# Two decode layers on one core: the last 2 KB of each row of three V loads per layer moved into short loads of their own

## The chip, the core and the metric

The kernel runs on one core of a Trainium2 chip. The metric is device time in microseconds (us), the median of several executions. A profiled execution gives the trace from which the durations below come.

## The reference

Two identical layers are run one after the other on a batch of four single tokens (decode): attention over a cache of 4096 keys and values, then a gated feed-forward block. Everything is float32.

```python
def _A_ref(x, k_cache, v_cache, wq, wo):          # x: 4 x 1 x 512
    q = (x @ wq).reshape(4, 1, 32, 128).transpose(0, 2, 1, 3)
    k = jnp.repeat(k_cache, 4, axis=1)             # k_cache, v_cache: 4 x 8 x 4096 x 128
    v = jnp.repeat(v_cache, 4, axis=1)
    scores = jnp.einsum("bhqd,bhkd->bhqk", q, k) * (128 ** -0.5)
    p = _softmax(scores, axis=-1)
    o = jnp.einsum("bhqk,bhkd->bhqd", p, v)
    return o.transpose(0, 2, 1, 3).reshape(4, 1, 4096) @ wo
def _B_ref(x, w1, w3, w2):                         # w1, w3: 512 x 1792, w2: 1792 x 512
    return (_silu(x @ w1) * (x @ w3)) @ w2
for _ in range(2):                                 # the same caches and weights in both layers
    x = x + _A_ref(_layernorm(x), k_cache, v_cache, wq, wo)
    x = x + _B_ref(_layernorm(x), w1, w3, w2)
```

The caches are by far the largest operands: K and V are 64 MB each, and both layers read both.

## The kernel before

The work of a layer runs over the eight KV heads, here called groups. For each group the core needs an 8 MB block of K and an 8 MB block of V. Each block is laid out in device memory as 128 rows of 64 KB, one row to a partition, so that one load (`nc.sync.dma_start`) fetches it whole. K block of group n gives the scores (`scores`, 32 matmuls of 512 columns on TensorE, L337); the softmax is taken from them (`factors`, `exponents`); V block of group n then gives the weighted sum (`weigh`, 32 matmuls on L380, in two halves of 16 with a copy of the first half by ScalarE between them, L387).

All loaded data lives in one SBUF tile, `arena`, 214 KB to a partition. A list `plan` holds every load of the program in order with the work that reads it. `pump` (L123 to L137) walks this list: as soon as room for the next entry is free in `arena` it writes the load into the program, always on SyncE (SP). `done` gives room back when the last reader of an entry has been written, and calls `pump` again. The order on SP is therefore the order of the plan, and SP works through it strictly in order: a load that must wait holds up every load behind it.

In the middle of layer 0 the arena holds one K block at 128 to 192 KB and one V block at 64 to 128 KB. The loads go K(n+1), V(n), K(n+2), V(n+1). K(n+1) may be issued when the scores of group n have read the K block that lies in its place, V(n) when `weigh` of group n-1 has read V(n-1). In layer 1 the groups run in reverse, 7 to 0, and the blocks of K move through the arena, but the alternation is the same.

Each load adds to a semaphore when its data has landed. SP's loads use eight such semaphores, DMAHW0 to DMAHW7, in turn. The program lets a load start only when the load that used the same semaphore before it, eight loads earlier, has landed. These waits, and those for room in `arena`, are what `[waits ...]` shows in the rows below (PE_49 is TensorE's own counter).

The line that issues the loads is L128:

```python
a = take(n, at)
if a is None:
    return
nc.sync.dma_start(arena[:, a * KB:(a + n) * KB], src)
```

Of the kernel before, what the change touches and what calls it, by code (L numbers as in the profile page):

```python
# [29 lines left out]
KB = 256  # L30
# [2 lines left out]
AGAIN = (0,)  # L33
SPLIT = 3
SCRATCH = 64


@with_exitstack
def tile_decode_layers(ctx: ExitStack, tc: tile.TileContext, x, kt, v, wq, wo, w1, w3, w2, out):
    nc = tc.nc  # L40
# [5 lines left out]
    arena = const.tile([P, ARENA * KB], F32, name="arena")  # L46
# [5 lines left out]
    def take(n, at=None):  # L52
        if at is not None and at < WO:
            return at
        for i, (lo, size) in enumerate(free):
            a = lo if at is None else at
            if lo <= a and a + n <= lo + size:
                free[i:i + 1] = [(p, s) for p, s in ((lo, a - lo), (a + n, lo + size - a - n)) if s]
                return a
        return None  # L60
# [60 lines left out]
    def pump():  # L121
        while state["next"] < len(plan):
            src, per, keys, at = plan[state["next"]]  # L123
            n = src.shape[-1] // KB
            a = take(n, at)
            if a is None:
                return
            nc.sync.dma_start(arena[:, a * KB:(a + n) * KB], src)  # L128
            i = state["next"]
            if i == 0:  # L130
                nc.sync.dma_start(xt[:8], x[:8])
            left[i] = (len(keys), a, n)
            for j, key in enumerate(keys):
                where[key] = (a + j * per, per, i)
            state["next"] += 1
# [5 lines left out]
    def done(*key):  # L141
        i = where[key][2]
        k, a, n = left[i]
        left[i] = (k - 1, a, n)
        if k == 1:
            give(a, n)
            pump()

    def vacate(*key):
        a, n, _ = where[key]  # L150
        give(a, n)
        pump()

    xt = const.tile([P, KC, B], F32, name="xt")
    nc.scalar.dma_start(xt[8:], x[8:])
    pump()

    ident = const.tile([P, P], F32, name="ident")
# [410 lines left out]
```

## Time and profile before

| | |
|---|---|
| time, median of 3 runs | 709.03 us (708.67 to 710.82) |
| the profiled execution | 710.14 us |
| its span, first to last instruction | 708.4 us |
| TensorE matmuls busy | 412.7 us, 58% of the span |
| VectorE / ScalarE busy | 78.0 us / 38.3 us |
| data moved by DMA | 299.89 MB in 13860 packets |
| mean granted TensorE clock | 0.793 |

How to read what follows: times are us from the start of the span unless marked ns. SPq is SP issuing. In the chain of waits a line is a start, a duration and what took that time; `DMA arena<-in_v` is a load of V, counted from its issue until the work that waited for it could go on. In a table by windows, each engine has its busy time and number of instructions, then come the granted TensorE clock, the mean busy share of the core's 16 DMA engines and the rate. A packet's whole time is put into the window in which it starts, so the share can come out over 1.00 in a short window. In the page's list of DMA issues a row gives the number of such loads, the KB of each and the median time from issue to landing.

### The profile page before, as it was taken

Reading aid. Unit: us, or ns where it says so; the run is one execution under the profiler, and the core shown is the slowest. Engines: PE = TensorE matmul, PEld = TensorE weight load, DVE = VectorE, ACT = ScalarE, POOL = GpSimd, SP = SyncE. Lnnn points to the kernel's source line nnn. Section 1 sums busy time; section 2 is a strip of 40 time slices with the busy share of each in tenths; the row PEclk is TensorE's granted clock in tenths of the full one; section 3 lists DMA queues with packets and bytes.
Section 4 is the critical chain, followed back from the end, with each engine's and each line's share of the span. In section 5 each row is a group of like instructions: output and inputs, shape, how many; then the busy total and the mean of one; then the engine's idle time right before and its main releaser. Section 6 shows DMA issues by size and latency. Waiting matters only on the chain.

```text
span 708.4 us, 7205 instructions
## 1 busy us (share of the span) xinstructions
PE 412.7 (58%) x3250; PEld 146.1 (21%) x3250; DVE 78.0 (11%) x270; ACT 38.3 (5%) x87; POOL 2.9 (0%) x10
## 2 busy tenths in 40 slices
PE   4455453546564564547778895365564645466677
PEld 2112021212121121212243321021121212121235
DVE  2001010101001000101011111010010101010111
ACT  0000000000000000002010000000000000000101
POOL 0000000000000000000000000000000000000000
PEclk9866687767778777778899998588797878788869
DMA  9999999999999999999999999999999999999996
GB/s 385 459 404 466 415 419 460 418 427 455 415 433 449 418 438 444 415 426 421 412 391 393 410 445 426 455 423 419 459 419 426 449 426 427 448 410 424 428 423 255
DMA packets 13860, 299.89 MB, mean 423 GB/s; under 512 B 1671, under 2 KB 1799, under 8 KB 6151
## 3 DMA queue, kind: packets, MB, share of 16 engines
q1 hardware_dynamic: 13696, 299.44, 98.9%
q8 instruction: 25, 0.41, 0.2%
q10 hardware_dynamic: 135, 0.01, 0.0%
q14 instruction: 4, 0.03, 0.0%
HBM read 299.38 MB, written 0.07 MB: 423 GB/s over the span
## 4 chain that ended last, share of the span: by engine, by line
DMA 73%; PE 22%; another core or an unknown queue 2%; ACT 1%; issue 1%; DVE 0%; SPq 0%; ACTq 0%
DMA arena<-in_v 52%; PE o_ps L380 16%; DMA arena<-in_w 9%; DMA arena<-in_wq 6%; DMA arena<-in_wo 3%; DMA arena<-in_kt 3%; PE s_ps L337 2%; PE q_ps L281 2%; ACT p L387 1%; PE m_ps L292 0%; PE t_ps L281 0%; PE x_ps L479 0%; SPq L128 0%; PE x_ps L401 0%
## 5 line engine op out<-in xcount | busy, mean ns | idle before, releaser
L380 PE MATMUL o_ps<-arena,pT 128*32 128x512 f32 x1024 | 150.6, 738 | 150.2 <-DMA arena<-in_v 136.6
L337 PE MATMUL s_ps<-arena,qpad 128*32 128x512 f32 x1024 | 149.7, 739 | 80.6 <-DMA arena<-in_kt 80.6
L380 PEld LDWEIGHTS o_ps<-arena,pT 128*32 128x32 f32 x1024 | 38.1, 131 | 259.7 <-issue 226.6
L337 PEld LDWEIGHTS s_ps<-arena,qpad 128*32 128x32 f32 x1024 | 39.4, 132 | 174.8 <-issue 161.7
L389 DVE SCALAR_TENSOR_TENSOR p<-o_ps,parts,p 128x512 f32<-128x512 f32 x16 | 12.0, 750 | 274.2 <-PE o_ps L380 249.2
L344 DVE TENSOR_REDUCE top<-s_ps 128x1 f32<-128x512 f32 x16 | 11.1, 691 | 191.8 <-PE s_ps L337 191.8
L392 PE MATMUL m_ps<-sel,p 128*128 128x16 f32 x128 | 17.0, 265 | 14.3 <-DVE p L389 14.2
L281 PE MATMUL q_ps<-arena,xpad 128*32 128x512 f32 x112 | 16.0, 696 | 11.6 <-DMA arena<-in_wq 11.6
L401 PE MATMUL x_ps<-arena,oT 128*4 128x256 f32 x256 | 18.7, 434 | 5.5 <-DMA arena<-in_wo 3.6
L392 PEld LDWEIGHTS m_ps<-sel,p 128*128 128x128 f32 x128 | 15.5, 191 | 29.2 <-DVE p L389 29.2
L387 ACT ACTIVATE p<-o_ps,parts 128x512 f32<-128x512 f32 x16 | 11.0, 687 | 193.4 <-PE o_ps L380 185.5
L368 PE MATMUL t_ps<-ident,p 128*128 128x128 f32 x64 | 10.9, 295 | 13.5 <-ACT p L362 13.5
L355 ACT ACTIVATE f<-d 128x1 f32<-128x1 f32 x16 | 3.2, 203 | 252.6 <-DVE d L353 252.6
L362 ACT ACTIVATE p<-s_ps,top 128x512 f32<-128x512 f32 x16 | 11.0, 684 | 81.7 <-PE m_ps L392 81.7
L225 PE MATMUL d_ps<-ident,rows 128*32 128x128 f32 x70 | 12.2, 277 | 0.0
L369 DVE COPY pT<-t_ps 128x512 f32<-128x512 f32 x16 | 11.1, 691 | 8.4 <-PE t_ps L368 8.4
L368 PEld LDWEIGHTS t_ps<-ident,p 128*128 128x128 f32 x64 | 7.0, 145 | 18.3 <-ACT p L362 15.3
L423 PE MATMUL s_ps<-arena,xpad 128*32 128x192 f32 (+1 forms) x128 | 9.3, 412 | 1.9 <-DMA arena<-in_w 1.5
L423 PE MATMUL o_ps<-arena,xpad 128*32 128x192 f32 (+1 forms) x128 | 8.1, 360 | 2.3 <-DMA arena<-in_w 2.2
L401 PEld LDWEIGHTS x_ps<-arena,oT 128*4 128x4 f32 x256 | 6.2, 94 | 14.4 <-issue 4.6
L225 PEld LDWEIGHTS d_ps<-ident,rows 128*32 128x32 f32 x70 | 7.5, 111 | 3.6
L281 PEld LDWEIGHTS q_ps<-arena,xpad 128*32 128x32 f32 x112 | 3.7, 126 | 21.6 <-DMA arena<-in_wq 12.7
(92 smaller groups left out, 130.4 us busy)
## 6 DMA issues: line engine op xcount, KB each, us to landing
arena<-in_kt SPq DMA_DIRECT2D x4, 4096.0 KB, 21.0
arena<-in_v SPq DMA_DIRECT2D x4, 4096.0 KB, 38.8
arena<-in_kt SPq DMA_DIRECT2D x9, 1024.0 KB, 10.2
arena<-in_w SPq DMA_DIRECT2D x15, 512.0 KB, 7.1
arena<-in_wq SPq DMA_DIRECT2D x1, 7168.0 KB, 39.5
arena<-in_v SPq DMA_DIRECT2D x3, 2048.0 KB, 39.3
arena<-in_wo SPq DMA_DIRECT2D x1, 4096.0 KB, 24.1
arena<-in_kt SPq DMA_DIRECT2D x2, 2048.0 KB, 19.9
```

What stands on the lines that cost most here:

```text
L225: nc.tensor.matmul(d_ps[0:32, :], rows, ident, start=True, stop=True)
L281: nc.tensor.matmul(ps[32 * k:32 * k + 32, :], xpad[:, k, lo:lo + 32], w[:, k, :], start=first, stop=last)
L337: nc.tensor.matmul(s_ps[32 * b:32 * b + 32, :], qpad[:, b, lo:lo + 32], k[:, j, :], start=(blk == 0), stop=(blk == NB - 1))
L344: nc.vector.tensor_reduce(top[:, 0:1], s_ps, axis=AX.X, op=ALU.max, negate=True)
L368: nc.tensor.transpose(t_ps[:, i, :], p[:, i * P:(i + 1) * P], ident)
L369: nc.vector.tensor_copy(pT.rearrange("p i r -> p (i r)"), t_ps.rearrange("p i r -> p (i r)"))
L380: nc.tensor.matmul(o_ps[32 * b:32 * b + 32, :], pT[:, i, 32 * b:32 * b + 32], w[:, b, :], start=(i == 0), stop=(i == NI - 1))
L387: nc.scalar.activation(p, o_ps, AF.Copy, scale=st["parts"][:, 0:1])
L389: nc.vector.scalar_tensor_tensor(p, o_ps, st["parts"][:, 1:2], p, op0=ALU.mult, op1=ALU.add)
L392: nc.tensor.matmul(flat(m), p[:, j * P:(j + 1) * P], sel[:, j].rearrange("p h b -> p (h b)"), start=(j == 0), stop=(j == 3))
L401: nc.tensor.matmul(x_ps[r:r + B, e * 256:e * 256 + 256], left(2 * i + n), w(n)[:, e * 256:e * 256 + 256], start=first, stop=last)
L423: nc.tensor.matmul(ps[32 * j:32 * j + 32, lo:lo + n], x32[:, k, :], w[:, j * n:(j + 1) * n], start=(k == 0), stop=(k == KC - 1))
```

## The change

A table `SHARES` names three V loads per layer: groups 2, 3 and 4 in layer 0 and groups 5, 4 and 3 in layer 1. For these, `pump` loads 62 KB of each row with the main load and the last 2 KB with short loads that each cover a run of rows: 15, 14, 13, 12, 10 and 64 rows for the first of the three; 11, 9, 7, 5 and 96 for the second; 8, 6, 4, 3, 2, 1, 8 and 96 for the third. They are written right behind the main load, on SP too. The bytes, their places in `arena` and all computation stay as they were.

```diff
+SHARES = {}
+for layer, groups in ((0, (2, 3, 4)), (1, (5, 4, 3))):
+    for g, c in zip(groups, ((15, 14, 13, 12, 10, 64), (11, 9, 7, 5, 96), (8, 6, 4, 3, 2, 1, 8, 96))):
+        SHARES["v", layer, g, 0] = c
...
-            nc.sync.dma_start(arena[:, a * KB:(a + n) * KB], src)
             i = state["next"]
+            rows_of = SHARES.get(keys[0], ())
+            m = n - 2 if rows_of else n
+            nc.sync.dma_start(arena[:, a * KB:(a + m) * KB], src[:, 0:m * KB])
+
+            r = 0
+            for c in rows_of:
+                nc.sync.dma_start(arena[r:r + c, (a + m) * KB:(a + n) * KB], src[r:r + c, m * KB:])
+                r += c
```

The first place is SP in layer 0, around the V load of group 4 (the third load of the three). Before, from V of group 3 on, then K5, V4, K6, V5, K7, V6:

```order
L128 DMA arena<-in_v 128x16384 [waits DMAHW5_49,DMAHW3_49,PE_49]
L128 DMA arena<-in_kt 128x16384 [waits DMAHW4_49,PE_49]
L128 DMA arena<-in_v 128x16384 [waits DMAHW5_49,PE_49]
L128 DMA arena<-in_kt 128x16384 [waits DMAHW6_49,PE_49]
L128 DMA arena<-in_v 128x16384 [waits DMAHW7_49,PE_49]
L128 DMA arena<-in_kt 128x16384 [waits DMAHW0_49,PE_49]
L128 DMA arena<-in_v 128x16384 [waits DMAHW1_49,PE_49]
```

K6 follows directly on V4 there. The same stretch of the changed program, K5, V4 with its eight short loads, K6, V5:

```order
L135 DMA arena<-in_kt 128x16384 [waits DMAHW2_49,PE_49]
L135 DMA arena<-in_v 128x15872 [waits DMAHW3_49,PE_49]
L139 DMA arena<-in_v 8x512 [waits DMAHW4_49,PE_49]
L139 DMA arena<-in_v 6x512 [waits DMAHW5_49]
L139 DMA arena<-in_v 4x512
L139 DMA arena<-in_v 3x512 [waits DMAHW6_49]
L139 DMA arena<-in_v 2x512 [waits DMAHW7_49]
L139 DMA arena<-in_v 1x512 [waits DMAHW0_49]
L139 DMA arena<-in_v 8x512 [waits DMAHW1_49]
L139 DMA arena<-in_v 96x512 [waits DMAHW2_49]
L135 DMA arena<-in_kt 128x16384 [waits DMAHW3_49,PE_49]
L135 DMA arena<-in_v 128x16384 [waits DMAHW4_49,DMAHW5_49,DMAHW2_49,DMAHW6_49,DMAHW1_49,DMAHW7_49,DMAHW0_49,PE_49]
```

K5 is counted on DMAHW1 here, V4's main load on DMAHW2 and the first seven short loads on DMAHW3 to DMAHW7, DMAHW0 and DMAHW1. The eighth short load, of 96 rows, comes round to DMAHW2 and waits on it; K6 stands behind that load. The other two V loads have five and six short loads, which do not come round to their own main load. In layer 1 the place looks the same at V of group 3: its eighth short load waits on the semaphore of its own main load, and the next K load stands behind it.

The second place is TensorE around `weigh` of the same group 4, which stands behind the scores of group 5. Before:

```order
L337 MATMUL s_ps<-arena,qpad 32x512 [waits DMAHW6_49,DVE_49]
L337 MATMUL s_ps<-arena,qpad 32x512 x31
L380 MATMUL o_ps<-arena,pT 32x512 [waits DMAHW7_49,DVE_49]
L380 MATMUL o_ps<-arena,pT 32x512 x15
L380 MATMUL o_ps<-arena,pT 32x512 [waits Activation_49]
L380 MATMUL o_ps<-arena,pT 32x512 x15
```

And in the changed program:

```order
L348 MATMUL s_ps<-arena,qpad 32x512 [waits DMAHW1_49,DVE_49]
L348 MATMUL s_ps<-arena,qpad 32x512 x31
L391 MATMUL o_ps<-arena,pT 32x512 [waits DMAHW2_49,DVE_49]
L391 MATMUL o_ps<-arena,pT 32x512 x15
L391 MATMUL o_ps<-arena,pT 32x512 [waits Activation_49]
L391 MATMUL o_ps<-arena,pT 32x512 x14
L391 MATMUL o_ps<-arena,pT 32x512 [waits DMAHW4_49,DMAHW5_49,DMAHW3_49,DMAHW6_49,DMAHW2_49,DMAHW7_49,DMAHW1_49,DMAHW0_49]
```

The last 2 KB of a row feed one matmul alone, the last of the 32 in `weigh`; it now waits for all the short loads, and the 31 before it wait for the main load only.

## The prediction, made before the changed kernel ran

> **What bounds the kernel now.** First the page's busy times and the chain that ended last.
>
> ```profile
> span 708.4 us, 7205 instructions
> PE 412.7 (58%) x3250; PEld 146.1 (21%) x3250; DVE 78.0 (11%) x270; ACT 38.3 (5%) x87; POOL 2.9 (0%) x10
> DMA packets 13860, 299.89 MB, mean 423 GB/s; under 512 B 1671, under 2 KB 1799, under 8 KB 6151
> q8 instruction: 25, 0.41, 0.2%
> DMA 73%; PE 22%; another core or an unknown queue 2%; ACT 1%; issue 1%; DVE 0%; SPq 0%; ACTq 0%
> ```
>
> No engine is busy for more than 58% of the span, while 73% of the chain is loads. The windows of three whole groups, the two in front of the third changed load of layer 0 and the one in front of that of layer 1, say how hard the loads run:
>
> ```profile
> core 0: us, PE busy (x) PEld busy (x) DVE busy (x) ACT busy (x) POOL busy (x), PEclk, DMA share, GB/s
> 159.50:198.20 38.70, 19.80 (x142) 6.44 (x142) 3.89 (x12) 1.67 (x4) 0.00 (x0) 0.76 1.00 434
> 198.20:236.90 38.70, 20.35 (x142) 6.55 (x142) 3.89 (x12) 1.67 (x4) 0.00 (x0) 0.76 1.00 434
> 540.60:579.30 38.70, 21.94 (x158) 7.03 (x158) 3.89 (x12) 1.67 (x4) 0.00 (x0) 0.76 1.00 432
> ```
>
> The DMA share is 1.00 and TensorE works 20 to 22 us of each 38.7 us. So the DMA engines are the bound, and a group costs the 16 MB that it moves at 434 GB/s. A microsecond in which they have nothing to do is a microsecond at the end. They never run dry, because the next load is queued long before the last one has landed:
>
> ```profile
> 209.16 0.33 SPq L128 DMA_DIRECT2D arena<-in_v  x1
> 226.30 0.33 SPq L128 DMA_DIRECT2D arena<-in_kt  x1
> 209.16 27.72 DMA arena<-in_v
> 236.89 0.14 issue
> 551.05 28.25 DMA arena<-in_v
> 569.02 0.33 SPq L128 DMA_DIRECT2D arena<-in_kt  x1
> ```
>
> The first two rows and the last are from the timeline, the others from the chain. V4 is issued at 209.16 and lands at 236.89; K6, behind it on SP, is issued at 226.30, so 236.89 - 226.30 = 10.6 us before V4 is in. V3 of layer 1 lands at 551.05 + 28.25 = 579.30, and the K load behind it was issued at 569.02, 10.3 us earlier. That lead keeps the share at 1.00.
>
> **The wait that the change adds.** In the changed program the eighth short load of these two V loads waits until its own main load has landed, since both use one semaphore, and the next K load stands behind it on SP. K6 can then be issued at 236.9 instead of 226.3. Everything issued earlier has landed by then: six of the other short loads were queued with V4, the seventh at K5's landing, one 8 MB load or 19 us before. So the DMA engines are empty from V4's last byte until the new issue brings bytes. This happens once a layer. The other V loads with five and six short loads reach back no further than to a load that landed a group ago.
>
> How long the engines stand empty is not shown before; the nearest rows are a load on an empty queue at the start and the store at the end:
>
> ```profile
> arena<-in_wq SPq DMA_DIRECT2D x1, 1024.0 KB, 4.9
> out<-p SPq DMA_DIRECT2D x1, 64.0 KB, 1.6
> 1.10:1.70 0.60, 0.00 (x0) 0.00 (x0) 0.36 (x1) 0.27 (x1) 0.21 (x1) 1.00 0.00 0
> 1.70:2.30 0.60, 0.00 (x0) 0.00 (x0) 0.56 (x7) 0.60 (x1) 0.00 (x0) 1.00 1.24 218
> 0.74 0.38 SPq L128 DMA_DIRECT2D arena<-in_wq  x1
> ```
>
> The gap consists of the time from last byte to landing plus that from issue to first byte, which is what issue to landing takes beyond moving the data. For the store it is 1.6 - 0.15 (64 KB at 434 GB/s) = 1.45 us; for the first load 4.9 - 2.4 (1 MB) = 2.5 us. The windows agree: issued at 0.74, no byte by 1.70, then only half the rate. The changed place is a load, but not the first of a program, so I take 1.9 us, between the two. The 0.33 us that SP needs for the 96-row load before it can issue K6 lies beside that load's own data, 192 KB or 0.45 us. **Two gaps: +3.8 us**, bounds +2.9 and +5.0.
>
> Nothing covers a gap. TensorE's slack doesn't help, as loads set the pace. TensorE itself isn't held by the short loads: the 31 matmuls before the last need the main load alone,
>
> ```profile
> 237.02 5.75 PE o_ps L380 x32
> 247.29 28.41 DMA arena<-in_v
> ```
>
> and `weigh` runs from 237.02 to 247.29, while the 96 rows land some 2.4 us after 236.9. If they came after 247 instead, V5's issue would slip too; 8 us of cover are left. V5 at 247.29 only queues behind K6.
>
> **The short loads themselves.** There are 6 + 5 + 8 = 19 more loads a layer. On a full queue the price of a small load shows where loads of 512 KB and 1 MB follow each other:
>
> ```profile
> 350.50:358.50 8.00, 7.50 (x114) 4.04 (x106) 0.94 (x5) 0.47 (x2) 0.00 (x0) 1.00 1.03 411
> 403.00:419.00 16.00, 13.14 (x102) 3.98 (x106) 2.97 (x10) 1.56 (x4) 0.00 (x0) 0.89 1.02 429
> L128 SPq DMA_DIRECT2D arena<-in_v x21: 327/328/432, 30.4 to 639.5; - x21
> ```
>
> 411 instead of 434 GB/s over 8 us is 0.42 us lost on 6.3 loads, 0.07 us a load; 429 over 16 us is 0.18 us on 6.5 loads, 0.03. Nineteen loads in two layers at most 0.07 each would be 2.7 us if every one occupied all engines, but 16 of 19 have at most 15 rows and touch only some; the three wide ones a layer give 6 x 0.03 to 0.07 = 0.2 to 0.4. I take **+0.2**, ends 0 and +1.0. SP's 0.33 us for each issue, 2.6 us for eight, lie inside the 17 us from V4's issue to K6's.
>
> **Who carries the rows.** A load of n rows below 16 can't occupy 16 engines evenly, so the short loads shift load between engines. At one row an engine, the 16 such loads of a layer give an engine 0 to 16 rows where an even split of their 128 rows gives 8. A 2 KB row costs 2 KB / (423/16 GB/s) = 0.08 us, so an engine gains or loses at most 0.62 us a layer. Whether that helps depends on who is late, and engines are apart:
>
> ```profile
> 700.00:701.00 1.00, 1.00 (x29) 0.81 (x32) 0.18 (x1) 0.00 (x0) 0.00 (x0) 1.00 0.61 244
> 701.00:702.00 1.00, 1.00 (x32) 0.97 (x28) 0.00 (x0) 0.00 (x0) 0.00 (x0) 1.00 0.46 178
> 703.00:704.00 1.00, 0.71 (x12) 0.47 (x13) 0.00 (x0) 0.00 (x0) 0.00 (x0) 1.00 0.13 47
> 704.00:704.60 0.60, 0.60 (x28) 0.60 (x24) 0.00 (x0) 0.00 (x0) 0.00 (x0) 1.00 0.09 34
> ```
>
> Behind the last load some engines are through before 701 and one or two run until 704.6, a lag of about 4 us; the 25 instruction fetches of q8, 16 KB each, are a likely source. No view names the late engines. If the short loads relieve them in both layers they gain 1.25 us; if they burden them they lose as much. I take **0**, ends -1.25 and +1.25.
>
> [...]
>
> A gap also makes all engines start level again. Lag that one engine had collected before it is paid there, and another may be last afterwards: at least 0, and at most about the price of a fetch or two a gap, 1.2 us (16 KB at 26 GB/s is 0.6). I take **+0.2** for both, ends 0 and +1.2.
>
> **The sum.** 3.8 + 0.2 + 0 + 0.2 = +4.2 us. On the profiled execution, span 708.4 and 710.14 in all (1.7 around the span), that is a span of 712.6. That execution lies 1.1 us over the median of 709.03; the forecast for the median is **709.0 + 4.2 = 713.2 us**. The ends of the terms together are 2.9 + 0 - 1.25 + 0 = +1.65 and 5.0 + 1.0 + 1.25 + 1.2 = +8.45.
>
> **Rivals.**
> 1. The gaps are there but short, about the store's 1.45 us each, and the shifted rows help a little: 2.9 - 1.0 = +1.9, 710.9 us, not to be told from no change (a measurement of this kernel tells 0.3%, 2.1 us). For it: the store's row. Against: a load has to fetch from device memory first. Chance 0.16.
> 2. Relief wins. The late engines are those with fewer rows, and the eighth load's wait finds its main load landed early enough that K6 is still queued in time: then -1.25, 707.8 us, not slower. It decides from the point at which V4 lands 2 us before the queue empties, which SP's order rules out, as nothing is queued behind V4. Chance 0.04.
> 3. Relief turns to burden: the late engines get more rows, lags don't carry over, gaps of 2.5: 5.0 + 1.25 + 1.0 + 0.8 = +8, 717 us. Chance 0.08.
> 4. Every short load costs its full latency on the path, 38 x 1.45 = 55 us, 764 us. For it: 38 loads under 200 KB. Against: in the 512 KB stage the rate stays at 411. Chance 0.01.
>
> [...]
>
> **How the numbers follow.** The forecast has 0.71, the rivals 0.16, 0.04, 0.08 and 0.01. The range goes from just below rival 1, 710.6, to 716.5, inside rival 3; about 2 in 10 are left out. Slower by over 0.3% (above 711.2): forecast, rivals 3 and 4, 0.80. Within 0.3%: rival 1 and most of 2, 0.18. Faster: 0.02.
>
> **What would show it.** In the trace after, K6's issue moves to V4's landing, some 11 us later than before, and the same for the K load behind V3 in layer 1; a window behind each of these landings has a DMA rate near 0 for one to two microseconds; from there on all landings are later by 2 us, then 4. The groups of the first and second changed V load run at 434 GB/s as before. TensorE's last matmul of `weigh` does not wait. The forecast is wrong if the rate doesn't fall there, if K6 is issued before the landing, or if landings slip elsewhere.

## The result, and the profile after

The change made the kernel slower: 720.31 us, the median of 4 runs (719.19 to 721.32), against 709.33 us before (4 runs, 708.67 to 710.82). That is +11.0 us, a ratio of 1.0155 (95% interval 1.014 to 1.017). The forecast was 713.2 us and its range ended at 716.5. The sign and the wait are as forecast. The size is not.

The page of the changed kernel, in its lines on the span, TensorE, the packets, the instruction fetches and the chain of waits:

```profile
span 719.5 us, 7273 instructions
PE 408.3 (57%) x3250; PEld 145.4 (20%) x3250; DVE 77.9 (11%) x270; ACT 38.3 (5%) x87; POOL 2.9 (0%) x10
DMA packets 14981, 299.90 MB, mean 417 GB/s; under 512 B 2023, under 2 KB 2151, under 8 KB 7271
q8 instruction: 25, 0.41, 0.2%
DMA 70%; PE 23%; another core or an unknown queue 3%; issue 2%; ACT 1%; DVE 1%; SPq 0%; POOLq 0%; ACTq 0%
```

The bytes are those of before (299.90 MB against 299.89), there are 25 instruction fetches again, TensorE's work has not grown, and most of the chain is still loads (70%). So 11 us went into moving the same bytes, at 417 instead of 423 GB/s. Where they went shows in SP's timeline (the first three rows and the sixth) and in the chain (the others), around the two waits:

```profile
210.83 0.35 SPq L135 DMA_DIRECT2D arena<-in_v  x1
211.27 28.22 SPq L139 DMA_DIRECT2D arena<-in_v  x8
239.59 0.37 SPq L135 DMA_DIRECT2D arena<-in_kt  x1
210.83 28.33 DMA arena<-in_v
249.32 33.00 DMA arena<-in_v
588.10 0.37 SPq L135 DMA_DIRECT2D arena<-in_kt  x1
559.33 28.33 DMA arena<-in_v
597.66 32.81 DMA arena<-in_v
```

V4 lands at 210.83 + 28.33 = 239.16. SP is at the eight short loads until 211.27 + 28.22 = 239.49, and only then issues K6, at 239.59 instead of 226.30. In layer 1 V3 lands at 587.66 and the K load follows at 588.10 instead of 569.02. So the wait stands where it was forecast.

The windows of the changed kernel show two groups that hold no such wait (from the landing of one changed V load to that of the next), the 2 us before V4's landing, and the 0.9 us behind each of the two waited landings:

```profile
159.78:199.82 40.04, 20.85 (x142) 6.65 (x142) 3.89 (x12) 1.67 (x4) 0.00 (x0) 0.71 1.00 421
508.56:548.65 40.09, 21.21 (x158) 6.85 (x158) 3.89 (x12) 1.67 (x4) 0.00 (x0) 0.80 1.00 416
237.00:238.00 1.00, 0.00 (x0) 0.00 (x0) 0.00 (x0) 0.00 (x0) 0.00 (x0) 0.50 0.03 8
238.00:239.00 1.00, 0.00 (x0) 0.00 (x0) 0.00 (x0) 0.00 (x0) 0.00 (x0) 0.50 0.05 14
239.20:240.10 0.90, 0.80 (x4) 0.23 (x8) 0.00 (x0) 0.00 (x0) 0.00 (x0) 0.50 0.00 0
587.70:588.60 0.90, 0.80 (x4) 0.23 (x8) 0.00 (x0) 0.00 (x0) 0.00 (x0) 0.50 0.00 0
```

The last two rows are the gaps: no packet starts. The two rows ahead of them show that the engines do not run dry all at once: from 237 on, 2 us before the landing, hardly a packet starts (8 and 14 GB/s). Spreading the bytes of each packet in the trace over the time that it took gives the whole course of this wait. 16 packets are under way until 236.2, then fewer and fewer; the last ends at 238.71 and the next starts at 240.11, so nothing moves for 1.4 us. By 241.5 there are 16 again, but for the next 2 us they move 361 GB/s instead of 434. Against 434 GB/s the three parts lose 1.5, 1.4 and 1.0 us, 3.8 in all, and the wait of layer 1 loses the same.

The first two rows were not forecast. Such a group took 38.7 us before and takes 40.0 to 40.1 now, with a DMA share still at 1.00. The engines always have a packet under way, but the packets take longer. The landings, each the sum of a start and a duration from the chain, put sizes to it:

| V load | landing before | after | later by |
|---|---|---|---|
| layer 0, V2 (first changed) | 159.49 | 159.78 | 0.3 |
| V3 | 198.18 | 199.82 | 1.6 |
| V4 (third, with the wait) | 236.88 | 239.16 | 2.3 |
| V5 | 275.70 | 282.33 | 6.6 |
| layer 1, V5 (first changed) | 501.90 | 508.56 | 6.7 |
| V4 | 540.60 | 548.65 | 8.1 |
| V3 (third, with the wait) | 579.30 | 587.66 | 8.4 |
| V2 | 618.01 | 630.47 | 12.5 |
| end of the span | 708.4 | 719.5 | 11.1 |

Two slips, of 4.3 and 4.1 us, stand behind the waits, as one behind a gap would, only larger than 1.9. (The after column has the landings of the main loads, which hold 256 KB, or 0.6 us, less than before. So 0.6 us of these two slips is bytes, and the rest agrees with the 3.8 above; and the first changed load is really 0.9 late, not 0.3.) The other slips stand where there is no wait.

### The profile page after: what moved, and what is told of

It is laid out like the page before. It is cut to its first block, busy times and chain, and to the rows that moved or that the text cites. A ratio compares the mean times of both kernels' runs of the same rounds, so it can differ in the third digit from the quotient of the medians.

```text
span 719.5 us, 7273 instructions
## 1 busy us (share of the span) xinstructions
PE 408.3 (57%) x3250; PEld 145.4 (20%) x3250; DVE 77.9 (11%) x270; ACT 38.3 (5%) x87; POOL 2.9 (0%) x10
## 2 busy tenths in 40 slices
DMA packets 14981, 299.90 MB, mean 417 GB/s; under 512 B 2023, under 2 KB 2151, under 8 KB 7271
## 4 chain that ended last, share of the span: by engine, by line
DMA 70%; PE 23%; another core or an unknown queue 3%; issue 2%; ACT 1%; DVE 1%; SPq 0%; POOLq 0%; ACTq 0%
DMA arena<-in_v 52%; PE o_ps L391 16%; DMA arena<-in_wq 5%; DMA arena<-in_w 5%; DMA arena<-in_kt 4%; DMA arena<-in_wo 3%; PE s_ps L348 2%; PE q_ps L292 1%; ACT p L398 1%; PE s_ps L434 1%; PE x_ps L490 0%; PE m_ps L274 0%; PE d_ps L236 0%; PE x_ps L412 0%
## 5 line engine op out<-in xcount | busy, mean ns | idle before, releaser
L391 PE MATMUL o_ps<-arena,pT 128*32 128x512 f32 x1024 | 147.6, 725 | 152.7 <-DMA arena<-in_v 140.5
L355 DVE TENSOR_REDUCE top<-s_ps 128x1 f32<-128x512 f32 x16 | 11.1, 691 | 204.3 <-PE s_ps L348 204.3
L380 DVE COPY pT<-t_ps 128x512 f32<-128x512 f32 x16 | 11.1, 691 | 8.3 <-PE t_ps L379 8.3
```

The lines of the kernel that those rows point to most:

```text
L355: nc.vector.tensor_reduce(top[:, 0:1], s_ps, axis=AX.X, op=ALU.max, negate=True)
L380: nc.vector.tensor_copy(pT.rearrange("p i r -> p (i r)"), t_ps.rearrange("p i r -> p (i r)"))
L391: nc.tensor.matmul(o_ps[32 * b:32 * b + 32, :], pT[:, i, 32 * b:32 * b + 32], w[:, b, :], start=(i == 0), stop=(i == NI - 1))
```

## The experiments

Each run was timed beside the kernel before on the same chip, and its times are differences of the two medians. Letters name theories within a group of runs and start anew in the next.

### Which part costs what

The first three runs take the change apart. Only the third V load of a layer has a wait, so the first run has none:

```diff
-    for g, c in zip(groups, ((15, 14, 13, 12, 10, 64), (11, 9, 7, 5, 96), (8, 6, 4, 3, 2, 1, 8, 96))):
+    for g, c in zip(groups, ((15, 14, 13, 12, 10, 64), (11, 9, 7, 5, 96), ())):
```

> The first and second of the three V loads of a layer keep their 11 short loads, the third is one load again; no load waits for its own main load. Theory A (each changed V load costs by itself about 1.2 us, on top of the wait): about half of what was measured before the waits, +4 to +5.5 us over the kernel before. Rival B (all of the +11 us comes from the two waits at the third loads, and the slips of 2.6 and 2.3 us seen ahead of them are paid back later): 0 to +1.5 us.

Measured: 714.02 against 708.86 us, +5.2 (ratio 1.0075, 1.0050 to 1.0100). The second has the third V load's short loads alone, with the wait:

```diff
+    for g, c in zip(groups, ((), (), (8, 6, 4, 3, 2, 1, 8, 96))):
```

> Only the third V load of a layer keeps its eight short loads, with the wait for its own main load. Theory A: two waits of 1.9 us and two changed loads of 1.2 us, +5.5 to +7 us. Rival B: nearly the whole of it, +9 to +11 us.

Measured: 714.74 us, +5.9 (1.0080, 1.0059 to 1.0100). 5.2 + 5.9 = 11.1 us is the whole change, so short loads without any wait carry nearly half of it: 5.2 us for four V loads, 1.3 each. The third run keeps all short loads of the change, but issues four of the third load's eight ahead of the main load. The ninth load, which comes round to the first one's semaphore, then finds it landed:

```diff
-            nc.sync.dma_start(arena[:, a * KB:(a + m) * KB], src[:, 0:m * KB])
...
-            for c in rows_of:
+            early = 4 if len(rows_of) == 8 else 0
+            for j, c in enumerate(rows_of + (0,)):
+                if j == early:
+                    nc.sync.dma_start(arena[:, a * KB:(a + m) * KB], src[:, 0:m * KB])
+                if not c:
+                    break
```

> All short loads of the change as they are, but four of the eight of the third V load are issued ahead of its main load, so that no short load comes round to the semaphore of its own main load and the next K load is issued while the main load is still streaming. Theory A: the two empty stretches go and the price of six changed loads stays, +6.5 to +8 us over the kernel before. Rival B: 0 to +2 us. In the trace the K load behind is issued 10 us ahead of the landing again.

Its SP timeline has K6 issued early again:

```profile
230.19 0.35 SPq L139 DMA_DIRECT2D arena<-in_kt  x1
```

Measured: 718.32 us, +9.5 (1.0134, 1.0103 to 1.0164), more than was expected. Without the waits most of the loss is still there, and the third V loads alone now cost 9.5 - 5.2 = 4.3 us, 2.1 each. By the two intervals that difference is good to about 3 us either way, and this run also puts four short loads ahead of the main load, which the change does not.

### Is it the small packets, the number of loads, or their unevenness?

The fourth run keeps the division into 62 KB and 2 KB of a row, but fetches the 2 KB of all 128 rows in one load:

```diff
+    for g, c in zip(groups, ((128,), (128,), (128,))):
```

> All six V loads are split at 62 KB, but the last 2 KB go with one load of 128 rows, eight rows to each engine. It tells what the price of a changed load hangs on. If it is the 2 KB packets in front of the next 64 KB rows: +5 to +7 us. If it is the number of short loads, or their uneven rows: 0 to +1.5 us.

Measured: 709.62 us, +0.8 (1.0009, 0.9999 to 1.0020). So neither the 2 KB packets nor a second load is to blame. The next two ask whether it is that the rows do not divide evenly over 16 engines, or a price for each load:

```diff
+    for g, c in zip(groups, ((16, 16, 16, 16, 32, 32),) * 3):
```

> All six V loads leave their last 2 KB to six short loads of 16, 16, 16, 16, 32 and 32 rows: as many loads as in the first set of the change, but every one spreads evenly over 16 engines. No load waits for its own main load. Theory A1 (short loads of fewer rows than engines, which leave the engines unequal, cost about 1.3 us for each changed V load): the price goes, 0 to +2 us over the kernel before. Rival A2 (each short load costs about 0.25 us on the queue whatever its rows): 36 loads, +7 to +9 us.

```diff
+    for g, c in zip(groups, ((8, 8, 112),) * 3):
```

> [...] Theory A1: most of the price of 1.3 us for each V load is there, +4 to +8 us. Rival A2: 18 loads at 0.13 to 0.25 us, +2.3 to +4.5 us. [...]

Measured: 718.03 us, +9.1 (1.0128, 1.0111 to 1.0145), and 717.55 us, +8.6 (1.0119, 1.0104 to 1.0134), both against 708.96. Six loads of 16 or 32 rows, which divide evenly, cost 9.1 / 6 = 1.5 us for a V load, and three loads, two of them with too few rows for 16 engines, 8.6 / 6 = 1.4. Both theories fall: loads that divide evenly are not free, and half as many loads cost the same.

Eight loads of 16 rows, in all six V loads and then in the third of each layer only, both with the wait:

```diff
+    for g, c in zip(groups, ((16,) * 8,) * 3):
```

> All six V loads leave their last 2 KB to eight short loads of 16 rows each; in each of the six the eighth waits for its own main load, so there are six waits instead of two. Under A1 the waits alone count: six times 1.5 to 2.2 us, +9 to +13 us. Under A2: those and 48 loads at 0.25, +21 to +25 us. If a wait costs little net (1 us or less, as the difference between the change and the run without the waits suggests): +4 to +7 us.

```diff
+    for g, c in zip(groups, ((), (), (16,) * 8)):
```

> Only the third V load of a layer is changed, into a main load and eight short loads of 16 rows each; the eighth waits for its own main load. The wait without uneven loads. Under A1: two waits of 1.5 to 2.2 us, +3 to +4.5 us. Under A2: two waits and 16 loads at 0.25, +7 to +8.5 us. If a wait costs 1 us or less net: +1.5 to +2.5 us.

Measured: 732.99 us, +24.0 (1.0348, 1.0323 to 1.0374) for six waits, 4.0 for each V load; and 715.24 us, +6.3 (1.0087, 1.0072 to 1.0102) for two, 3.1 each. The first lies in the range of the price by the load (+21 to +25), which the run with three loads contradicts; the second lies between the ranges of the two theories. It is close to the +5.9 of the change's own third sets, so with a wait too it hardly matters how the rows are divided.

### The places of the rows

One thing is left that sets the harmless run with one 128-row load apart: the short loads of all others cover rows that are neighbours. Four loads of 32 rows that each take every fourth row, then four of 32 neighbours, and two of 64:

```diff
+    for g, c in zip(groups, ((32, 32, 32, 32),) * 3):
...
-                nc.sync.dma_start(arena[r:r + c, (a + m) * KB:(a + n) * KB], src[r:r + c, m * KB:])
-                r += c
+                nc.sync.dma_start(arena[r::4, (a + m) * KB:(a + n) * KB], src[r::4, m * KB:])
+                r += 1
```

> All six changed V loads have their tail in four loads of 32 rows, and each takes every fourth row, so that its rows lie spread over all 128 partitions. No load waits for its own main load. Theory A (places): short loads cost because their rows are neighbours, so that all engines write into the same few partitions and hold each other up; spread rows then cost little, 0 to +3 us over before. Rival B (rows to an engine): a load that gives each engine one or two rows costs whatever partitions it goes to; +6 to +9 us, as for the even loads of 16 and 32 neighbouring rows (+9.1).

> As the run with four spread loads of 32 rows in all six V loads, but the 32 rows of a load are neighbours. Theory A (places): clearly more than the spread loads, +4 to +9 us over before. Rival B (rows to an engine): the same as the spread loads, +6 to +9 us.

```diff
+    for g, c in zip(groups, ((64, 64),) * 3):
```

> All six changed V loads have their tail in two loads of 64 neighbouring rows, four rows to an engine. Theory A (places): a load still reaches only half of the partitions, so it costs, +3 to +9 us over before. Rival B (rows to an engine): four rows to an engine are nearly the eight of the single 128-row tail (+0.8), so +0.8 to +1.5 us.

Measured against 708.92 us: spread rows 709.48, +0.6 (1.0009, 0.9999 to 1.0018); neighbours 719.05, +10.1 (1.0142, 1.0124 to 1.0159); halves 718.57, +9.7 (1.0140, 1.0120 to 1.0161). The same 24 loads of 32 rows cost 0.6 or 10.1 us, by which rows they take alone. The rival, that few rows to an engine cost wherever they go, is out, and with it any price for a load as such that would matter here (24 of them cost 0.6 us). A group between two changed V loads, first of the run with spread rows, then of the one with 32 neighbours:

```profile
159.03:197.82 38.79, 20.79 (x142) 6.66 (x142) 3.89 (x12) 1.67 (x4) 0.00 (x0) 0.72 1.00 433
506.17:547.01 40.84, 21.60 (x158) 6.94 (x158) 3.89 (x12) 1.67 (x4) 0.00 (x0) 0.75 1.01 419
```

The group with spread rows runs at the rate of before, the other loses 2 us with its DMA share no lower.

With spread rows the wait can be priced alone: eight loads of 32 spread rows by 1 KB in the third V load of each layer, the eighth of which waits for its main load as in the change.

```diff
+    for g, c in zip(groups, ((), (), (32,) * 8)):
...
-                nc.sync.dma_start(arena[r:r + c, (a + m) * KB:(a + n) * KB], src[r:r + c, m * KB:])
-                r += c
+                x0, f = m * KB + r // 4 * KB, r % 4
+                nc.sync.dma_start(arena[f::4, a * KB + x0:a * KB + x0 + KB], src[f::4, x0:x0 + KB])
+                r += 1
```

> Only the third changed V load of each layer: eight tail loads of 32 rows by 1 KB, each over every fourth row, and the eighth waits for its own main load as in the change. Theory A (places): the short loads cost next to nothing and the two waits are left alone, two times 1.9 us and some, +3 to +4.5 us over before. Rival B (rows to an engine): the price of the short loads, about 1.4 us for each of the two V loads, comes on top, +6 to +7 us.

Measured: 714.58 us, +5.7 (1.0089, 1.0063 to 1.0116), or 2.8 a wait. That is between the two theories' ranges, and the interval, 4.5 to 8.2 us, touches both. In its trace, a row of SP's timeline, two of the chain, and the window behind V4's landing:

```profile
236.76 0.53 SPq L135 DMA_DIRECT2D arena<-in_kt  x1
209.23 26.95 DMA arena<-in_v
247.12 32.44 DMA arena<-in_v
236.20:237.70 1.50, 1.39 (x8) 0.45 (x12) 0.00 (x0) 0.00 (x0) 0.00 (x0) 0.50 0.10 21
```

V4's main load lands at 236.18 and K6 is issued at 236.76. For 1.5 us behind the landing the rate is 21 GB/s, which is the eighth short load. V5 lands at 279.56, so 43.4 us after V4, against 38.8 before. 0.6 of the difference is the 256 KB that V4's main load no longer holds; the wait took 4.0. By the waited load of layer 1 part of that has come back:

```profile
551.99 28.37 DMA arena<-in_v
```

It lands at 580.36, 1.1 us later than before (579.30), or 1.7 with the 0.6 us of bytes that this main load lacks, and the span ends 712.6 - 708.4 = 4.2 us later. So a wait costs 4 us at its place and 2 to 3 in the end.

### Written places or read places?

In those runs the places in SBUF and in device memory changed together. Six runs tell them apart: the kernel before, with one extra load behind each of the six V loads, of the last 2 KB of some rows once more, into a part of the arena that is idle then and that nothing reads. There is no new wait. First 64 source rows into partitions 0 to 63, then the same 64 source rows into partitions 32 to 95:

```diff
             nc.sync.dma_start(arena[:, a * KB:(a + n) * KB], src)
+            if keys[0][:3] in (("v", 0, 2), ("v", 0, 3), ("v", 0, 4), ("v", 1, 5), ("v", 1, 4), ("v", 1, 3)):
+                nc.sync.dma_start(arena[0:64, 192 * KB:194 * KB], src[0:64, 62 * KB:64 * KB])
```

> The kernel before with one extra load behind each of the six V loads: the last 2 KB of 64 neighbouring rows (128 KB) once more, into partitions 0 to 63 of an unused part of the arena that nothing reads. No new wait. The bytes alone are 6 x 0.3 = 1.8 us. [...]

```diff
+                nc.sync.dma_start(arena[32:96, 192 * KB:194 * KB], src[0:64, 62 * KB:64 * KB])
```

> [...] Rival B (source, or neighbours as such): the same as with partitions 0 to 63, +5 to +11 us.

Measured against 709.30 us: 717.01, +7.7 (1.0112, 1.0096 to 1.0127), and 711.12, +1.8 (1.0028, 1.0018 to 1.0038). Two groups of layer 1 in each, first with partitions 0 to 63, then with 32 to 95:

```profile
505.21:546.04 40.83, 22.52 (x158) 7.13 (x158) 3.89 (x12) 1.67 (x4) 0.00 (x0) 0.75 1.00 418
546.04:586.40 40.36, 22.64 (x158) 7.13 (x158) 3.89 (x12) 1.67 (x4) 0.00 (x0) 0.75 1.01 419
```

```profile
502.22:541.43 39.21, 22.66 (x158) 7.10 (x158) 3.90 (x12) 1.67 (x4) 0.00 (x0) 0.76 1.00 432
541.43:580.48 39.05, 20.99 (x158) 6.78 (x158) 3.90 (x12) 1.67 (x4) 0.00 (x0) 0.81 1.01 435
```

The same bytes are read from the same places. Moved by 32 partitions they cost their bytes alone, 38.7 + 0.3 = 39.0 us a group (39.2 and 39.1 measured); not moved, 1.3 to 1.6 us more. This settles it: the price hangs on the partitions that are written.

Beyond its bytes a load into partitions 0 to 63 costs (7.7 - 1.8) / 6 = 1.0 us. What sets these 64 partitions apart from 32 to 95 is not shown.

Then an extra load of 16 rows (32 KB) into partitions 0 to 15, and one of 32 neighbouring source rows (64 KB) into every fourth partition:

```diff
+                nc.sync.dma_start(arena[0:16, 192 * KB:194 * KB], src[0:16, 62 * KB:64 * KB])
```

> [...] The bytes alone are 6 x 0.08 = 0.5 us. [...] Rival C (price by the bytes): a quarter of what 64 rows cost, +1 to +3 us.

```diff
+                nc.sync.dma_start(arena[0::4, 192 * KB:194 * KB], src[0:32, 62 * KB:64 * KB])
```

> [...] The bytes alone are 6 x 0.15 = 0.9 us. [...] Rival B (source): neighbouring source rows cost as elsewhere, +5 to +10 us.

Measured: 711.46 us, +2.2 (1.0030, 1.0019 to 1.0041), and 709.89, +0.6 (1.0009, 0.9999 to 1.0018). Spread partitions are free again, with neighbouring source rows. Sixteen rows cost (2.2 - 0.5) / 6 = 0.28 us beyond their bytes, about a quarter of what 64 cost: the price goes by the rows (or their bytes, as all rows here are 2 KB), not by the load, as rival C has it.

Last, wide loads, 112 rows into partitions 16 to 127 and 96 into 32 to 127:

```diff
+                nc.sync.dma_start(arena[16:128, 192 * KB:194 * KB], src[16:128, 62 * KB:64 * KB])
```

> The kernel before with one extra load behind each of the six V loads, as in the other runs with an extra load, here 112 rows (224 KB) into partitions 16 to 127. The bytes alone are 6 x 0.53 = 3.2 us. [...]

```diff
+                nc.sync.dma_start(arena[32:128, 192 * KB:194 * KB], src[32:128, 62 * KB:64 * KB])
```

> The same with 96 rows (192 KB) into partitions 32 to 127, as the widest short load of the change. The bytes alone are 6 x 0.45 = 2.7 us. [...]

Measured against 708.85 us: 719.58, +10.7 (1.0149, 1.0132 to 1.0166), and 718.89, +10.0 (1.0146, 1.0131 to 1.0162). Beyond their bytes that is 1.3 and 1.2 us a load. So a load that covers most of the partitions costs as well, while 64 rows into 32 to 95 cost their bytes alone: how many partitions a load covers does not decide it. A 2 KB row in a load that costs takes 1.3 / 112 = 11 ns to 0.28 / 16 = 18 ns more than the 5 ns that it takes at 434 GB/s.

The packets of the traces show who pays. A packet here is one row of a load. Take those of 62 or 64 KB that start between 150 and 245 us, a stretch with three of the six V loads. Their median is 2.42 us in all these runs. In the kernel before, 2 of them take longer than 2.6 us; with spread rows and with partitions 32 to 95 it is 2 again, and there no 2 KB packet takes longer than 0.085 us. With partitions 0 to 63 it is 68, the longest 3.50 us, nearly all within a few us of the extra loads, and with 112 rows 67. What the 66 additional ones take beyond 2.42 us adds up to 39.6 us of engine time, 39.6 / 16 / 3 = 0.8 us a load on each of 16 engines, most of the 1.0 that was measured. So the price is paid by rows of the 8 MB loads that are under way beside the short ones, and hardly by the short rows themselves. They do meet: the rows of the first extra load start over a stretch of 2.6 us (157.31 to 159.93), so some engines are at them while others are still at the main load or already at the next one. But a packet of the trace names neither its engine nor its partition, so why the large rows then take longer is not shown.

## Why the prediction was wrong, step by step

**What bounds the kernel** held. TensorE's busy time did not grow (412.7 us before, 408.3 after), and what the loads lost came out at the end (11.1 us of span).

**Two gaps, +3.8 us, and the lag, +0.2.** The place was right: K6 moved from 226.30 to 239.59, and from V4's landing to V5's issue at 249.32, behind `weigh`, it is 10.2 us (10.4 before), so the last matmul did not wait. The empty stretch was sized too high if anything: 1.4 us without a packet where 1.9 was taken, so 2.8 for two, just under the lower bound of 2.9. What was missing lies on both sides of it. The prediction let all engines fall empty at V4's last byte; in the trace they ran out one after another from 3 us before the landing (1.5 us lost), and started slowly afterwards (1.0). The first is the lag between engines, which the prediction named and put at 0.2. A wait thus took 3.8 us at its place, and some of it came back later: the run with the wait alone gives 5.7 us in the end (interval 4.5 to 8.2), where the two terms had 4.0 and an upper end of 5.0 + 1.2 = 6.2. What brings it back, no run isolates.

**The short loads themselves, +0.2 us.** This is the step that failed. They cost 5.2 us in the first two V loads of a layer alone, where the prediction's end for all of them was 1.0. It took their price from 512 KB and 1 MB loads, 0.03 to 0.07 us a load, and those rows were of 128 partitions each. It then argued that loads of few rows cost less because they occupy few engines. The runs showed the opposite: 128 rows in one load cost 0.8 us in six V loads, the same rows in each division into neighbours that was run without a wait 8.6 to 10.1 us. What matters is which partitions a load writes, and most of the cost falls on the large rows beside it; the rows of the trace from which the prediction took its price hold no such case. The sentence that the groups of the first and second V load would run at 434 GB/s was wrong with it: the groups behind the first ones run at 421 and 416. That landings slip where there is no wait is one of the signs that the prediction itself had named for being wrong.

**Who carries the rows, 0.** The term asked how many rows an engine gets. Six even loads cost 1.5 us a V load and three uneven ones 1.4, so that was not the question to ask.

**The sum.** By the runs: 5.7 for the waits, 5.2 for the short loads of the first two V loads, and 5.9 - 5.7 = 0.2 that the third ones add beside a wait, 11.1 us; measured 11.0. That it comes out so closely is partly luck, as the 0.2 is good to 2 or 3 us only. The parts do not seem to add in the third V loads: without the wait their short loads cost 4.3 us, with it 0.2 beyond the wait. The traces agree with that. In the 6 us behind each waited landing, 15 and 15 of the large packets take over 2.6 us in the changed kernel, and 16 and 13 in the run with spread rows, so nothing there tells the change's short loads from spread ones. Why a wait hides their price is not shown.

**The rivals.** None was this one. Rival 4, a full latency for each short load, would have been 764 us, and the run with 24 loads of spread rows at 0.6 us rules out a price by the load. Rival 3's 717 us was the nearest in size, for another reason.

## What to carry to other kernels

On a full DMA queue, price a small load by the partitions it writes before its size: here rows into all 128 partitions, into every fourth or into 32 to 95 cost their bytes, while 2 KB rows in the other runs of neighbours tried (0 to 15, 0 to 63, 16 to 127 and 32 to 127 among them) cost some 10 to 18 ns each on top of 5, whatever number of loads they were cut into. A row of a trace prices another load only if it writes the same kind of place. And when loads take their semaphores in turn, count how many are issued behind a load that must not be waited for: the one that comes round to its semaphore empties the queue, 2 to 3 us a time here.

## What the runs showed of the hardware

- Extra or tail loads of 128 rows, of 32 rows into every fourth partition and of 64 rows into 32 to 95 were free beyond their bytes, at most 0.13 us a V load. The other extra loads cost 0.28 us each for 16 rows into 0 to 15, 1.0 for 64 rows into 0 to 63, 1.2 for 96 rows into 32 to 127 and 1.3 for 112 rows into 16 to 127. What the partitions of the free loads have in common is not shown.
- The price falls on the large rows beside the short ones: some 22 of the 64 KB packets around an extra load into partitions 0 to 63 took over 2.6 and up to 3.50 us instead of 2.42, and none beyond those of before with 32 to 95.
- The DMA share does not show it. It is 1.00 in the group at 434 GB/s and in those at 416 to 421; only the rate tells, or the time from landing to landing.
- An emptied queue cost 3.8 us at its place, of which only 1.4 had no packet under way: 1.5 went while the engines ran out one after another, and 1.0 in a restart at 361 GB/s. One to two us of it came back later in the program.
